# Last sliding-window layer: value products split by past and own keys, the last tile's scores in two bursts, its residual on two engines with one store, and new instruction orders

## The chip, the cores and the metric

One core of one Trainium2 chip runs the whole program. The metric is the device time of one execution in microseconds (us). The engines are named as in the profile: PE (TensorE, matrix products; PEld its weight loads), DVE (VectorE), ACT (ScalarE), POOL (GpSimd), SP (SyncE, which issues most DMAs).

## The reference

Four layers follow each other on x of 2048 tokens by 512 features, in bf16; each normalises x, computes an attention block and adds it to x. Layers 1 and 3 are a linear attention (A), layers 2 and 4 a softmax attention over a sliding window of 256 keys (B), both with 32 heads of 16 features. The last layer is a B layer:

```
def _B_ref(x, wqkv, wo):
    H = 32; Dh = D // H; W = 256
    q, k, v = ...                      # x @ wqkv, split by head
    scores = einsum("bhqd,bhkd->bhqk", q, k) * (Dh ** -0.5)
    mask = (idx[:, None] - idx[None, :] >= 0) & (idx[:, None] - idx[None, :] < W)
    p = _softmax(where(mask, scores, -1e9))
    return einsum("bhqk,bhkd->bhqd", p, v) ... @ wo

x = x + _A_ref(_layernorm(x), A_wqkv, A_wo)
x = x + _B_ref(_layernorm(x), B_wqkv, B_wo)
x = x + _A_ref(_layernorm(x), A_wqkv, A_wo)
x = x + _B_ref(_layernorm(x), B_wqkv, B_wo)
```

## The kernel before

The 2048 tokens are 16 tiles of 128. x stays in the on-chip memory (`xres`) through all four layers. In a B layer the loop of `middle` goes over the tiles j. For each tile it projects queries, keys and values some tiles ahead, and then works on key blocks: a tile has two blocks of 64 keys (2j and 2j + 1), and the 128 output partitions of a score matmul are the 64 keys of a block for two heads.

- `b_scores` (L623): one burst of eight score matmuls for two of the four head groups f and one key block b. The matmuls use a quarter of the rows of the array each (tile_position), so that a burst writes four accumulation banks. Keys of a tile meet the queries of the same and of the next tiles, so that the scores come out transposed, keys on partitions. Two ScalarE exponentials (L648) take the burst to `pb` or `vp` (the buffer `K.P`), and masks follow on DVE (L658) or POOL (L657). For tile 15, which has no later queries, a burst is 128 columns (b = 0) or 64 (b = 1) per head group.
- `b_far` (L682, exponentials L692, masks L702, L710, L711): the far edge of the window, for tiles with j + 2 < 16.
- `b_values` (L716, matmuls L731): value products of tile j, for h = 0 and 1, two steps "pv" of 24 matmuls each. A matmul takes 128 queries of one head pair against one key block, over up to six blocks: the two own ones first and then up to four past ones. The 34 output columns hold for each of two heads 16 features and a column for the softmax sum; a reciprocal (L742) and a multiplication (L743) give `o`.
- `b_out` (L748): transpose of `o` by a DMA (or, where `by_pe`, by TensorE), four products of 512 columns with `wBo` (L406), and the residual on DVE (L574); then a store of the tile (L849). The last tile has `b_last` (L755): transposes by TensorE in two halves (L766), products (L777), two half residuals on DVE (L783) and a store after each (L784).

The order of the instructions is not computed in the kernel. `place` (L92) reads a compressed table of numbers that gives, for every step, its rank, its engine where it may run on two, and its accumulation bank. `synchronise` puts in the semaphore waits. Every engine works through its own queue in this order.

## Time and profile before

| | |
|---|---|
| median of 3 runs | 407.9 us (407.73 to 408.55) |
| the profiled execution | 409.79 us; span 408.1 us |
| busy share of the span | PE 95%, ACT 84%, DVE 82%, PEld 64%, POOL 37% |
| last ACT exponential of the program | 397.99 + 1.87 us, the last of a row of four |
| granted TensorE clock, mean | 0.999 |

The span runs from the first to the last instruction; the time of an execution also has what lies around it. In the group rows, "busy, mean ns of one | idle before, releaser" is read as: the engine was busy for so long on this group, one instruction took so long, and it stood idle so long just before instructions of the group, mostly for the one named. In the timeline rows the first two numbers are start and length.

### The profile page before, as it was taken

To read this page: it belongs to the slowest core of one execution; us is meant where nothing else is said; L and a number is where in the kernel's file an instruction comes from. 1 tells how busy PE (TensorE), PEld (TensorE's weight loads), DVE (VectorE), ACT (ScalarE), POOL (GpSimd) and SP (SyncE) were. 2 spreads that over 40 slices of the span, in tenths; PEclk is the share of its full clock that TensorE was granted. 3 is DMA by queue.
4 is the path that set the end of the run, shared out by engine and by line. 5 is a ranking of instruction groups with operands and counts; after the bars stand their busy time and mean duration, and the time that the engine had idled before them with its cause. 6 is when DMAs were issued, how large, how long until landed. Compare 5 with 4: busy or idle time off the path is not lost.

```text
span 408.1 us, 18068 instructions
## 1 busy us (share of the span) xinstructions
PE 386.1 (95%) x7922; PEld 262.9 (64%) x7997; DVE 333.4 (82%) x758; ACT 341.3 (84%) x441; POOL 151.6 (37%) x246
## 2 busy tenths in 40 slices
PE   8999999998999999999999999999999999899895
PEld 4544776766575566565665777676767766576663
DVE  5998898979998898887857789988798768776774
ACT  3465569998999999999998345999899999999992
POOL 3555624443464455451742223132313223030351
PEclk9999999999999999999999999999999999999999
DMA  7934316333263535343232000345214433345352
GB/s 247 243 65 103 106 41 136 106 77 85 69 95 81 120 83 113 75 116 93 60 72 41 16 2 27 98 100 126 65 46 121 109 89 74 74 111 115 83 146 81
DMA packets 67654, 37.88 MB, mean 93 GB/s; under 512 B 48248, under 2 KB 62712, under 8 KB 67576
## 3 DMA queue, kind: packets, MB, share of 16 engines
q1 hardware_dynamic: 67184, 35.67, 36.6%
q8 instruction: 63, 1.03, 1.1%
q0 software_dynamic: 384, 1.05, 0.7%
q14 instruction: 15, 0.12, 0.1%
q10 hardware_dynamic: 8, 0.00, 0.0%
HBM read 6.29 MB, written 2.10 MB: 21 GB/s over the span
## 4 chain that ended last, share of the span: by engine, by line
PE 69%; ACT 12%; DVE 9%; DMA 5%; issue 2%; SPq 1%; ACTq 0%
PE ps L406 22%; PE ps L420 18%; PE ps L731 14%; ACT pb L648 9%; PE ps L638 7%; DMA xres<-in_A_x_dram 2%; PE ps L682 2%; DMA pb<-in_B_wqkv_dram 2%; DVE stats L367 1%; DVE vp L431 1%; PE ps L679 1%; ACT vp L648 1%; PE ps L457 1%; ACT pb L692 1%; DVE o L743 1%
## 5 line engine op out<-in xcount | busy, mean ns | idle before, releaser
L648 ACT ACTIVATE pb<-ps 128x1024 bf16<-128x1024 f32 (+3 forms) x224 | 198.4, 973 | 8.1 <-PE ps L638 6.6
L731 PEld LDWEIGHTS ps<-vB,pb 128*128 128x128 bf16 x2560 | 77.7, 96 | 11.2 <-issue 5.0
L731 PE MATMUL ps<-vB,pb 128*128 128x34 bf16 x2560 | 83.1, 177 | 1.0 <-issue 0.8
L420 PE MATMUL ps<-xT,wBp 128*128 128x128 bf16 x1024 | 68.8, 219 | 0.3 <-ACT pb L648 0.3
L420 PEld LDWEIGHTS ps<-xT,wBp 128*128 128x128 bf16 x1024 | 58.7, 98 | 10.6 <-issue 4.6
L710 POOL TENSOR_SCALAR_AFFINE_SELECT pb<-pb 128x1024 bf16<-128x1024 bf16 x35 | 40.4, 1155 | 64.0 <-DVE pb L702 37.2
L429 ACT ACTIVATE tE<-ps 128x512 bf16<-128x512 f32 x64 | 37.8, 605 | 24.6 <-PE ps L406 15.0
L692 ACT ACTIVATE pb<-ps 128x1024 bf16<-128x1024 f32 x50 | 49.3, 1052 | 2.1 <-PE ps L682 1.0
L657 POOL TENSOR_SCALAR_AFFINE_SELECT pb<-pb 128x512 bf16<-128x512 bf16 x50 | 33.7, 674 | 45.0 <-ACT pb L648 18.1
L574 DVE TENSOR_TENSOR xres<-ps,xres 128x512 bf16<-128x512 f32 x63 | 42.8, 682 | 9.3 <-PE ps L406 9.0
L638 PE MATMUL ps<-XQ,kB 32*128 32x256 bf16 (+2 forms) x1024 | 48.1, 262 | 2.2 <-ACT pb L648 0.8
L370 POOL TENSOR_TENSOR rs<-ve,negh 128x1 f32<-128x1 f32 x64 | 37.0, 578 | 32.1 <-DVE ve L369 27.5
L406 PE MATMUL ps<-wA,XQ 128*128 128x512 bf16 x179 | 45.9, 379 | 2.8 <-DMA XQ<-vp 0.8
L367 DVE BATCH_NORM_STATS2 stats<-xres 128x6 f32<-128x512 bf16 x64 | 43.7, 685 | 3.1 <-DMA xres<-in_A_x_dram 2.3
L420 PE MATMUL ps<-XQ,wA 128*128 128x128 bf16 x512 | 35.4, 219 | 0.1
L369 POOL TENSOR_SCALAR ve<-mv 128x1 f32<-128x1 f32 x45 | 11.3, 252 | 63.2 <-DVE mv L368 61.1
L420 PEld LDWEIGHTS ps<-XQ,wA 128*128 128x128 bf16 x512 | 30.5, 98 | 5.9 <-issue 0.7
L638 PEld LDWEIGHTS ps<-XQ,kB 32*128 32x128 bf16 x1024 | 15.4, 92 | 27.6 <-ACT pb L648 9.3
L742 DVE RECIPROCAL rc<-ps 128x16 f32<-128x16 f32 x64 | 16.1, 252 | 20.2 <-PE ps L731 19.7
L406 PE MATMUL ps<-wBv,xT 128*128 128x512 bf16 x108 | 30.1, 380 | 2.4 <-issue 1.3
L406 PE MATMUL ps<-wBo,oT 128*128 128x512 bf16 x103 | 28.5, 380 | 3.0 <-issue 1.8
L406 PE MATMUL ps<-M,XQ 128*128 128x512 bf16 x114 | 29.7, 380 | 1.3 <-issue 0.6
(116 smaller groups left out, 562.0 us busy)
## 6 DMA issues: line engine op xcount, KB each, us to landing
vB<-vS SPq DMA_DIRECT2D x64, 136.0 KB, 2.6
kB<-vp SPq DMA_DIRECT2D x64, 128.0 KB, 2.4
wA<-in_A_wqkv_dram SPq DMA_DIRECT2D x3, 512.0 KB, 5.2
xres<-in_A_x_dram SPq DMA_DIRECT2D x2, 512.0 KB, 4.8
pb<-in_B_wqkv_dram SPq DMA_DIRECT2D x1, 1024.0 KB, 8.6
out_dram<-xres POOLq DMA_DIRECT2D x8, 128.0 KB, 2.7
out_dram<-xres SPq DMA_DIRECT2D x7, 128.0 KB, 2.9
xres<-in_A_x_dram SPq DMA_DIRECT2D x3, 256.0 KB, 4.9
```

The source lines that it names most:

```text
L367: self.on("DVE", "stats", lambda e: e.bn_stats(K.stats[:, t, :], K.xres[:, t, :]), key, dve(512), rd=[("xres", t)], wr=[("stats", t)])
L370: self.pow = self.on("POOL", "pow", lambda e: e.tensor_tensor(K.rs[:, t, :], K.ve[:, t, :], K.negh[:], ALU.pow), key + 0.03, (640, 690), r ...
L406: m = e.matmul(K.ps(ps), lhs(c), rhs(c), start=c == 0, stop=c == 3)
L420: m = e.matmul(K.ps(ps)[:, f * P:(f + 1) * P], w(c, f), xT(c), start=c == 0, stop=c == 3)
L429: self.on("ACT", "E", lambda e: e.activation(K.tE[:, s, :], K.ps(ps), ACT.Exp, bias=0.0), key, act(512), wr=[("tE", s)], ps=[ps])
L574: self.on("DVE", "res", lambda e: e.tensor_tensor(K.xres[:, t, :], K.ps(po), K.xres[:, t, :], ALU.add), key, dve(512), rd=[("xres", t)], w ...
L638: m = e.matmul(K.ps(ps[gq])[:, ns * i:ns * i + ns], K.kB[rows, j % 4, 2 * f + b, :, :], K.XQ[rows, f, q:q + ns], start=True, stop=True, ti ...
L648: return e.activation(out(h, ns).rearrange("p (f g) c -> p f g c", f=n), i, ACT.Exp, bias=0.0, scale=0.25)
L657: return e.affine_select(out=x, in_=x, compare_op=ALU.is_ge, fill=0.0, base=1, pattern=[[0, 4 * n], [2, 64]], channel_multiplier=-1)
L692: return e.activation(o.rearrange("p (f g) b c -> p f g b c", g=2), i, ACT.Exp, bias=0.0, scale=0.25)
L710: return e.affine_select(out=x, in_=x, compare_op=ALU.is_ge, fill=0.0, base=-2, pattern=[[0, 16], [-2, 64]], channel_multiplier=1)
L731: m = e.matmul(K.ps(ps)[:, 34 * u:34 * u + 34], K.P((b // 2) % rp)[:, f, gq % 2 * 2 + gq // 2, o:o + P], K.vB[:, (b // 2) % 4, b % 2, r, : ...
```

## The change

Only the last layer changes. Its steps become:

- From tile 1 on the value products of two head groups are split in two each: those of the four past key blocks (16 matmuls) and those of the two own ones (8), in the same bank. The past part depends on the scores of earlier tiles alone (`b_split`).
- Tile 15's scores come in two bursts, one for each pair of head groups, with both key blocks side by side in a bank (192 columns for each group): two exponentials of 768 columns for each burst, and four masks, all on DVE (`b_scores_end`). Its own-key products are split by which of the two exponentials they need (`b_values_end`).
- In `b_last` the right half of x of tile 15 is added on TensorE, by a product with the identity, and copied out by ScalarE; the left half is added on DVE; one store of 128 KB follows both.
- `pe_last3` = 2: tile 14's `o` is also transposed by TensorE and no longer by a DMA.
- The table is new. Up to the last layer's first projections all engines have the same instructions in the same order as before; from there order, engines of copies and masks, and banks differ.

```
@@ -25,7 +25,7 @@
...
-    k_ao3=3.649, k_kv3=2.494, k_v3=-0.211, pe_first3=3, pe_last3=1, o_bke3=-0.456, o_res3=2.95,
+    k_ao3=3.649, k_kv3=2.494, k_v3=-0.211, pe_first3=3, pe_last3=2, o_bke3=-0.456, o_res3=2.95,
...
@@ -214,6 +214,7 @@
 
 LATE = 5
 FILL = 10
+SPLIT = 1
 
 
 def bass_view(x, free):
@@ -659,6 +660,39 @@
 
         self.g.add("mk", {"DVE": dve(256 * n, "2x"), "POOL": (600, 660)}, mk, key + 0.02, rd=[("P", sl, f, b, h) for f in fs for h in range(2)] + [("tri",)], wr=[("P", sl, f, b, 2) for f in fs])
 
+    def b_scores_end(self, j, fs, key):
+
+        K = self
+        ps = [Tile(1, "S") for _ in range(4)]
+        w = 3 * P // 2
+        span = lambda two, free: bass_view(K.PS[:, two[0].banks[0], :], free([512 * (two[1].banks[0] - two[0].banks[0]), 2]))
+
+        def put(e):
+            m = None
+            for i, f in enumerate(fs):
+                for b in range(2):
+                    c, q = w * i + 64 * (1 - b), P * j + 64 * b
+                    for gq in range(4):
+                        rows = slice(32 * gq, 32 * gq + 32)
+                        m = e.matmul(K.ps(ps[gq])[:, c:c + P - 64 * b], K.kB[rows, j % 4, 2 * f + b, :, :], K.XQ[rows, f, q:P * j + P], start=True, stop=True, tile_position=(32 * gq, 0))
+            return m
+
+        self.pe("s", put, key, 1, w * len(fs), mode=(32, 128), rd=[("kB", j % 4, 0), ("kB", j % 4, 1), ("XQ", j)], ps=ps)
+        sl = j % self.rp
+        for h in range(2):
+            def ex(e, h=h):
+                i = span(ps[2 * h:2 * h + 2], lambda x: [[w, 2], x, [1, w]])
+                o = bass_view(K.P(sl)[:, fs[0], h, 384:384 + w], [[1408, 4], [1, w]])
+                return e.activation(o.rearrange("p (f g) c -> p f g c", f=2), i, ACT.Exp, bias=0.0, scale=0.25)
+
+            self.on("ACT", "ex", ex, key + 0.01 * h, act(4 * w), wr=[("P", sl, f, b, h) for f in fs for b in range(2)], rd=[("P", sl, f) for f in fs], ps=[ps[2 * h], ps[2 * h + 1]])
+        for h in range(2):
+            def mk(e, h=h):
+                x = bass_view(K.P(sl)[:, fs[0], h, 384:448], [[1408, 4], [64, 2], [1, 64]])
+                return e.tensor_tensor(x, x, K.tri[:, 0, :].unsqueeze(1).unsqueeze(1).to_broadcast([P, 4, 2, 64]), ALU.mult)
+
+            self.on("DVE", "mk", mk, key + 0.02 + 0.01 * h, dve(512, "2x"), rd=[("P", sl, f, b, h) for f in fs for b in range(2)] + [("tri",)], wr=[("P", sl, f, b, 2, h) for f in fs for b in range(2)])
+
     def b_far(self, j, key):
 
         K = self
...
-    def b_values(self, j, h, key):
+    def b_whole(self, j, h, key, ps):
+
         K = self
         rp = self.rp
-        ps = Tile(1, K.cls)
...
+    def b_split(self, j, h, key, ps):
+
+        K = self
+        rp = self.rp
+        prior = [(2 * j - 1, 64), (2 * j - 2, 128), (2 * j - 3, 192), (2 * j - 4, 256)][:2 * j]
+        own = [(2 * j, 0), (2 * j + 1, -64)]
+        fs = (2 * h, 2 * h + 1)
+        parts = [(f, prior, f == fs[0], 0) for f in fs if prior] + [(f, own, f == fs[0] and not prior, 1) for f in fs]
+        for f, blocks, first, late in parts:
+            def put(e, f=f, blocks=blocks, first=first):
+                m = None
+                for gq in range(4):
+                    r = 4 * f + gq
+                    u = 4 * (f - 2 * h) + gq
+                    for i, (b, c) in enumerate(blocks):
+                        o = 384 * (b % 2) + c
+                        m = e.matmul(K.ps(ps)[:, 34 * u:34 * u + 34], K.P((b // 2) % rp)[:, f, gq % 2 * 2 + gq // 2, o:o + P], K.vB[:, (b // 2) % 4, b % 2, r, :], start=first and gq == 0 and i == 0, stop=blocks is own, skip_group_check=True)
+                return m
...
+            self.pe("pv", put, key - 0.4 * (1 - late) - 0.001 * (f % 2), 4 * len(blocks), 34, rd=rd, ps=[ps])
+
+    def b_values(self, j, h, key):
+        K = self
+        rp = self.rp
+        ps = Tile(1, K.cls)
+        if not (self.merged and j >= SPLIT):
+            self.b_whole(j, h, key, ps)
+        else:
+            self.b_split(j, h, key, ps)
         s = j % 2
         v = lambda: K.ps(ps)[:, 0:272].rearrange("p (u a d) -> p u a d", u=8, a=2)
         self.on("DVE", "rcp", lambda e: e.reciprocal(K.rc[:, s, h, :].rearrange("p (u a) -> p u a", a=2), v()[:, :, :, 16]), key + 0.02, dve(16, "recip"), wr=[("rc", s, h)], ps=[ps])
@@ -745,6 +814,51 @@
             v()[:, :, :, 0:16], K.rc[:, s, h, :].rearrange("p (u a) -> p u a", a=2).unsqueeze(3).to_broadcast([P, 8, 2, DH]), ALU.mult),
             key + 0.03, dve(256), rd=[("rc", s, h)], wr=[("o", s, h)], ps=[ps])
 
+    def b_values_end(self, j, h, key):
+
+        K = self
+        rp = self.rp
+        ps = Tile(1, K.cls)
+        fs = (2 * h, 2 * h + 1)
+        prob = lambda b, f, gq: K.P((b // 2) % rp)[:, f, gq % 2 * 2 + gq // 2, :]
+        val = lambda b, f, gq: K.vB[:, (b // 2) % 4, b % 2, 4 * f + gq, :]
+        for f in fs:
+            def put(e, f=f):
+                m = None
+                for gq in range(4):
+                    u = 4 * (f - 2 * h) + gq
+                    for b, c in ((2 * j - 4, 256), (2 * j - 3, 192), (2 * j - 2, 128), (2 * j - 1, 64)):
+                        o = 384 * (b % 2) + c
+                        m = e.matmul(K.ps(ps)[:, 34 * u:34 * u + 34], prob(b, f, gq)[:, o:o + P], val(b, f, gq), start=f == fs[0] and gq == 0 and b == 2 * j - 4, stop=False, skip_group_check=True)
+                return m
+            rd = []
+            for i in (j - 2, j - 1):
+                rd += [("P", i % rp, f)] + [("vB", i % 4, a, b) for a in range(2) for b in range(2)]
+                rd += [("P", i % rp, f, b, h_) for h_ in range(3) for b in (0, 1)]
...
+            self.pe("pv", put, key - 0.4 - 0.001 * (f % 2), 16, 34, rd=rd, ps=[ps])
+        for k in range(2):
+            def put(e, k=k):
+                m = None
+                for f in fs:
+                    for gq in (2 * k, 2 * k + 1):
+                        u = 4 * (f - 2 * h) + gq
+                        x = prob(2 * j, f, gq)
+                        e.matmul(K.ps(ps)[:, 34 * u:34 * u + 34], x[:, 448:576], val(2 * j, f, gq), start=False, stop=False, skip_group_check=True)
+                        m = e.matmul(K.ps(ps)[:, 34 * u:34 * u + 34], x[:, 320:448], val(2 * j + 1, f, gq), start=False, stop=True, skip_group_check=True)
+                return m
+            rd = [("vB", j % 4, a, b) for a in range(2) for b in range(2)]
+            for f in fs:
+                rd += [("P", j % rp, f)] + [("P", j % rp, f, b, k) for b in (0, 1)] + [("P", j % rp, f, b, 2, k) for b in (0, 1)]
+            self.pe("pv", put, key - 0.001 * (1 - k), 8, 34, rd=rd, ps=[ps])
...
     def b_out(self, j, key, by_pe):
         K = self
         s = j % 2
@@ -775,13 +889,14 @@
                     m = None
                     for f in (h, h + 2):
                         m = e.matmul(K.ps(po)[:, cs], K.oT[:, s, f, :], K.wBo[:, f, cs], start=f == 0, stop=f == 3, skip_group_check=True)
+                    if h == 0:
+                        m = e.matmul(K.ps(po)[:, 256:512], K.ident[:], K.xres[:, j, 256:512], start=False, stop=False, skip_group_check=True)
                     return m
 
-                self.pe("bout", put, key + 0.1 * h + 0.01 * (n or 0), 2, cs.stop - cs.start, rd=[("oT", s, h), ("wBo",)], ps=[po])
-        for n in range(2):
-            cs = slice(256 * n, 256 * n + 256)
-            self.on("DVE", "res", lambda e, cs=cs: e.tensor_tensor(K.xres[:, j, cs], K.ps(po)[:, cs], K.xres[:, j, cs], ALU.add), key + 0.2 + 0.1 * n, dve(256), rd=[("xres", j)], wr=[("xres", j, n)], ps=[po])
-            self.on("SP", "out", lambda e, cs=cs: e.dma_start(K.out[0, j * P:(j + 1) * P, cs], K.xres[:, j, cs]), key + 0.3 + 0.1 * n, (520, 2400), rd=[("xres", j, n)])
+                self.pe("bout", put, key + 0.1 * h + 0.01 * (n or 0), 2 if h else 2.5, cs.stop - cs.start, rd=[("oT", s, h), ("wBo",), ("xres", j), ("ident",)], ps=[po])
+        self.on("ACT", "res", lambda e: e.activation(K.xres[:, j, 256:512], K.ps(po)[:, 256:512], ACT.Copy), key + 0.2, act(256), rd=[("xres", j)], wr=[("xres", j, 1)], ps=[po])
+        self.on("DVE", "res", lambda e: e.tensor_tensor(K.xres[:, j, 0:256], K.ps(po)[:, 0:256], K.xres[:, j, 0:256], ALU.add), key + 0.2, dve(256), rd=[("xres", j)], wr=[("xres", j, 0)], ps=[po])
+        self.on("SP", "out", lambda e: e.dma_start(K.out[0, j * P:(j + 1) * P, :], K.xres[:, j, :]), key + 0.3, (520, 2400), rd=[("xres", j, 0), ("xres", j, 1)])
 
     def phase(self, ph):
 
@@ -831,12 +946,15 @@
             if j + 1 < T:
                 self.b_v(j + 1, (j + 1) % ring, base + j + 1 - par["k_v"])
             for f in (0, 2):
+                if last and j == T - 1:
+                    self.b_scores_end(j, [f, f + 1], base + j + f / 4)
+                    continue
                 for b in range(2):
                     self.b_scores(j, b, [f, f + 1], base + j + (f + b) / 4)
             if j + 2 < T:
                 self.b_far(j, base + j + 0.8)
             for h in range(2):
-                self.b_values(j, h, base + j + (h + 1) / 2 + par["k_pv"])
+                (self.b_values_end if last and j == T - 1 else self.b_values)(j, h, base + j + (h + 1) / 2 + par["k_pv"])
             if not last:
                 self.closing = [self.g.ops[-1]]
             k = base + j + 1 + par["k_wo"]
@@ -859,60 +977,61 @@
 
 
 TABLE = (
-    r"c-qxkW1u8i(hXg;ZQHhO+qP}nwr$(CZQGpb9`~2|YG!tOwtKf1f4;2B%&NE%anCssbzf%Hd*U9uXYRQJAV7HF!T>`kP!J9TG$e#X5E{Zm1V{`?ASon+<Y3^T",
...
+    r"c-qx@W1uWawsmYo?1;LyZCib9+qP|6-Pg8l+qP|6eQms~Q{6M&)3<wi-n{R}S5=vLYRAS}Yez<A)`{th;fw8y<5LP1sHncsid0CYRanK!s01pZ3Z=rS@G6l?",
...
```

The first place is TensorE's queue over the scores of tiles 14 and 15. Rows are equal instructions that follow each other; L638 (before), L639 and L677 (after) are score matmuls, L731, L791 and L832 value products, L406 and L407 output products, `pb` and `vp` the exponentials' buffers. Before:

```order
L638 MATMUL ps<-XQ,kB 128x256 x8
L406 MATMUL ps<-wBo,oT 128x512 x4
L731 MATMUL ps<-vB,pb 128x34 x24
L638 MATMUL ps<-XQ,kB 128x64 x8
L731 MATMUL ps<-vB,pb 128x34 x24
L638 MATMUL ps<-XQ,kB 128x128 x8
L731 MATMUL ps<-vB,pb 128x34 x48
L638 MATMUL ps<-XQ,kB 128x64 x8
L406 MATMUL ps<-wBo,oT 128x512 x2
L638 MATMUL ps<-XQ,kB 128x128 x8
```

After:

```order
L639 MATMUL ps<-XQ,kB 128x256 x8
L407 MATMUL ps<-wBo,oT 128x512 x2
L791 MATMUL ps<-vB,pb 128x34 x32
L677 MATMUL ps<-XQ,kB 128x128 x4
L677 MATMUL ps<-XQ,kB 128x64 x4
L677 MATMUL ps<-XQ,kB 128x128 x4
L677 MATMUL ps<-XQ,kB 128x64 x4
L791 MATMUL ps<-vB,pb 128x34 x64
L677 MATMUL ps<-XQ,kB 128x128 x4
```

The four small bursts of tile 15 stood between blocks of 24 and 48 value products; now the first of two comes after 32 products of tile 14's past keys, and 64 products, own and past, stand ahead of the second.

The second place is the end of DVE's queue: masks (L658; L692 after), reciprocals (L742; L856), divisions (L743; L857), residuals of a whole tile (L574; L575) and of half of tile 15 (L783; L898). Before:

```order
L658 TENSOR_TENSOR vp<-vp,tri 128x8x64
L742 RECIPROCAL rc<-ps 128x16
L743 TENSOR_TENSOR o<-ps,rc 128x8x2x16
L742 RECIPROCAL rc<-ps 128x16
L743 TENSOR_TENSOR o<-ps,rc 128x8x2x16
L574 TENSOR_TENSOR xres<-ps,xres 128x512 x2
L783 TENSOR_TENSOR xres<-ps,xres 128x256 x2
```

After:

```order
L692 TENSOR_TENSOR vp<-vp,tri 128x4x128 x4
L856 RECIPROCAL rc<-ps 128x16
L857 TENSOR_TENSOR o<-ps,rc 128x8x2x16
L856 RECIPROCAL rc<-ps 128x16
L857 TENSOR_TENSOR o<-ps,rc 128x8x2x16
L575 TENSOR_TENSOR xres<-ps,xres 128x512
L396 COPY oT<-ps 128x2x128
L575 TENSOR_TENSOR xres<-ps,xres 128x512
L898 TENSOR_TENSOR xres<-ps,xres 128x256
```

All four masks of tile 15 now stand together ahead of both reciprocals, a copy of the transposed second half of tile 15 has come between the two whole residuals, and one half residual has left for ScalarE.

The third place is the end of TensorE's queue (L731, L847, L848 value products, L766, L880 transposes, L777, L891 tile 15's output products, L893 the product with the identity). Before:

```order
L731 MATMUL ps<-vB,pb 128x34 x4
L777 MATMUL ps<-wBo,oT 128x512 x2
L766 MATMUL ps<-ident,o 128x128 x2
L406 MATMUL ps<-wBo,oT 128x512 x4
L777 MATMUL ps<-wBo,oT 128x256 x4
```

After:

```order
L848 MATMUL ps<-vB,vp 128x34
L407 MATMUL ps<-wBo,oT 128x512 x4
L880 MATMUL ps<-ident,o 128x128 x2
L407 MATMUL ps<-wBo,oT 128x512 x2
L880 MATMUL ps<-ident,o 128x128 x2
L407 MATMUL ps<-wBo,oT 128x512 x2
L891 MATMUL ps<-wBo,oT 128x512 x2
L893 MATMUL ps<-xres,ident 128x256
L891 MATMUL ps<-wBo,oT 128x256 x4
```

The output products of tile 13 (the first four of L407) have moved behind the last value products, and tile 15's first half of output products behind those of tile 14.

121 lines of the change are left out of this document (68 added, 53 removed).

## The prediction

> **What bounds the kernel now.** I read the page first, then the busy time by stretches, then the groups of one engine, then the engines' rows over the last ten microseconds.
>
> ```profile
> span 408.1 us, 18068 instructions
> PE 69%; ACT 12%; DVE 9%; DMA 5%; issue 2%; SPq 1%; ACTq 0%
> ```
>
> The chain of waits is mostly TensorE over the whole program, but only the last layer changes, so that layer has to be read alone. Its first score exponentials start at 256.8 us and its last one ends at 399.86 us. The busy time by stretches, with the columns named in the first line:
>
> ```profile
> core 0: us, PE busy (x) PEld busy (x) DVE busy (x) ACT busy (x) POOL busy (x), PEclk, DMA share, GB/s
> 256.80:290.00 33.20, 32.16 (x704) 22.61 (x710) 28.63 (x68) 31.98 (x42) 8.47 (x11) 1.00 0.41 104
> 290.00:340.00 50.00, 47.72 (x1212) 33.78 (x1220) 40.30 (x91) 46.15 (x59) 12.49 (x15) 1.00 0.35 87
> 340.00:399.86 59.86, 54.96 (x1610) 40.10 (x1620) 42.88 (x100) 57.85 (x73) 18.09 (x24) 1.00 0.44 104
> 399.86:408.10 8.24, 3.92 (x72) 2.51 (x70) 3.75 (x9) 0.77 (x2) 0.56 (x1) 0.96 0.28 80
> ```
>
> Up to 340 us TensorE (96%) and ScalarE (94%) are both nearly full. From 340 us ScalarE is busy 97% and TensorE 92%: the exponentials set the pace. Over the three stretches ScalarE is busy 135.98 of 143.06 us, so 7.1 us of idle time is all that an order can win there. The last 8.24 us belong to nobody: a chain of short steps. The ScalarE groups between 256.8 and 399.86 us say what the engine does and what it waits for:
>
> ```profile
> L648 ACT ACTIVATE pb<-ps 128x896 bf16<-128x896 f32 x88 | 74.6, 937 | 3.0 <-PE ps L638 3.0
> L692 ACT ACTIVATE pb<-ps 128x1024 bf16<-128x1024 f32 x22 | 21.7, 1045 | 1.3 <-PE ps L682 1.0
> L648 ACT ACTIVATE vp<-ps 128x896 bf16<-128x896 f32 x24 | 20.6, 944 | 1.0 <-PE ps L638 1.0
> L692 ACT ACTIVATE vp<-ps 128x1024 bf16<-128x1024 f32 x6 | 5.8, 1021 | 0.9 <-PE ps L682 0.8
> L648 ACT ACTIVATE pb<-ps 128x768 bf16<-128x768 f32 x4 | 3.1, 849 | 0.0
> L395 ACT ACTIVATE XQ<-ps 128x512 bf16<-128x512 f32 x5 | 3.1, 611 | 0.1
> L648 ACT ACTIVATE vp<-ps 128x512 bf16<-128x512 f32 x4 | 2.2, 595 | 0.2
> L648 ACT ACTIVATE vp<-ps 128x256 bf16<-128x256 f32 x4 | 1.4, 431 | 0.4 <-PE ps L638 0.4
> L395 ACT ACTIVATE vS<-ps 128x512 bf16<-128x512 f32 x2 | 1.3, 658 | 0.0
> L591 ACT ACTIVATE vp<-ps 128x512 bf16<-128x512 f32 x1 | 0.8, 762 | 0.0
> L548 ACT ACTIVATE rec<-recf 128x128 bf16<-128x128 f32 x2 | 0.6, 306 | 0.0
> ```
>
> Nearly all of the idle time, 3.0 + 1.3 + 1.0 + 0.9 + 0.4 = 6.6 us, is an exponential that waits for its burst of score matmuls (L638, L682). So what matters is how early TensorE reaches a burst, how many instructions ScalarE has, and how long the last chain is.
>
> **Part 1, the last tile's scores in two bursts.** Today the last tile has four bursts and eight exponentials, four of 512 columns and four of 256. They stand in these two ScalarE rows (start, length):
>
> ```profile
> 395.65 1.96 ACT L648 ACTIVATE vp<-ps 128x256 bf16<-128x256 f32 x4
> 397.99 1.87 ACT L648 ACTIVATE vp<-ps 128x256 bf16<-128x256 f32 x4 [0.39 <-PE ps L638]
> ```
>
> That is 1.96 + 1.87 = 3.83 us. They become four of 768 columns; the four of that size above took 3.1 us together. Gain 0.7 us, all of it on the engine that sets the pace. The wait of 0.39 us between the groups I leave in: in the new order TensorE has 64 value products between the two new bursts. Forty-eight of them take 1.37 us by the row below, so 64 take about 1.75 us, while ScalarE has at that point one 1024-column and two 768-column exponentials before it, about 2.5 us. The burst and the mask that the last of these products wait for use up the rest, and 0.2 to 0.4 us of waiting remains.
>
> ```profile
> 396.40 1.37 PE L731 MATMUL ps<-vB,pb 128*128 128x34 bf16 x48
> ```
>
> **Part 2, copies that change engines.** In the new order ScalarE loses, between the 9th and the 85th exponential of the layer, two query copies net (0.61 each), one value copy (0.66) and two of the reciprocals' copies (0.31 each) and gains one key copy (0.76): 1.22 + 0.66 + 0.61 - 0.76 = 1.7 us less. All of this lies before 340 us or little after it, where TensorE is as full as ScalarE, so it need not show. Its bounds are 0 and 1.7 us; I take 0.7, since TensorE sets the pace there about as often as ScalarE. VectorE pays: about four us more with the masks that also move to it, on 111.8 busy us of 143.1. That is 81% instead of 78%, so it is hidden as long as no burst waits for it.
>
> **Part 3, value products split.** The number of products does not change: 24 for a group of four heads before, 16 + 8 after. Only their place does. Products of past keys no longer wait for the tile's own exponentials and masks, and blocks of 24 to 48 between two bursts become blocks of 8 to 64. No row prices that. The upper bound of the gain is the 6.6 us of burst waits; the loss has no bound in the trace, and the nearest row is the same 6.6 us once more. Since the two orders hold the bursts and the projections in nearly the same places, I take 0.5 us of gain.
>
> **Part 4, the end.** The rows after the last exponential (399.86 us), first VectorE, then TensorE, ScalarE and the SP queue:
>
> ```profile
> 399.89 0.43 DVE L658 TENSOR_TENSOR vp<-vp,tri 128x512 bf16<-128x512 bf16 x1 [1.37 <-ACT vp L648]
> 401.92 0.26 DVE L742 RECIPROCAL rc<-ps 128x16 f32<-128x16 f32 x1 [0.97 <-PE ps L731]
> 402.21 0.42 DVE L743 TENSOR_TENSOR o<-ps,rc 128x256 bf16<-128x256 f32 x1
> 403.88 0.69 DVE L574 TENSOR_TENSOR xres<-ps,xres 128x512 bf16<-128x512 f32 x1 [0.65 <-PE ps L406]
> 404.49 0.87 DVE L783 TENSOR_TENSOR xres<-ps,xres 128x256 bf16<-128x256 f32 x2
> ...
> 400.38 0.21 PE L731 MATMUL ps<-vB,vp 128*128 128x34 bf16 x2
> 401.63 0.25 PE L731 MATMUL ps<-vB,pb 128*128 128x34 bf16 x4
> 402.69 0.28 PE L766 MATMUL ps<-ident,o 128*128 128x128 bf16 x2 [0.32 <-DVE o L743]
> 402.81 1.03 PE L406 MATMUL ps<-wBo,oT 128*128 128x512 bf16 x4
> 403.68 0.60 PE L777 MATMUL ps<-wBo,oT 128*128 128x256 bf16 x4
> ...
> 403.01 0.38 ACT L395 ACTIVATE oT<-ps 128x256 bf16<-128x256 bf16 x1 [1.31 <-PE ps L766]
> ...
> 403.26 1.67 SPq L849 DMA_DIRECT2D out_dram<-xres  x2
> 404.97 0.92 SPq L784 DMA_DIRECT2D out_dram<-xres  x2
> ```
>
> Now, counted from the last exponential: the mask, then 48 products (400.38 to 401.88), then reciprocal and division, ready at +2.77; then one residual, the transposes, eight products with the output weights and three more residual steps, the last ready at 405.36, that is +5.5; then the second half store.
>
> After: the mask ends at about +0.55 (three masks queue up behind each other), and only 8 of the last 32 own-key products wait for it, 0.2 us and 0.2 until their result is there: +1.0. Two pairs of reciprocal and division follow each other on VectorE, 0.71 us each by the rows 401.92 to 402.63, from +0.8: ready at +2.2, so 0.55 earlier. Then VectorE has the residual of tile 13 (0.69), a copy of the transposed tile (about 0.38, as ScalarE's), the residual of tile 14 (0.69) and one half residual (0.43): +4.4. TensorE has, from +1.0, eight output products of 512 columns for tiles 13 and 14 (1.03 for four in the row 402.81, so 2.0), two transposes, two products of 512 and one of 256 and four of 256 (0.60): its last result comes at about +4.2, and ScalarE's half residual (about 0.4) ends at +4.6. So the last residual is ready 0.9 us earlier. The extra product with the identity (256 columns) lies beside VectorE's residuals and costs nothing; uncovered it would cost 0.1 us.
>
> The store becomes one of 128 KB instead of two of 64 KB, of which only the second is at the end. Medians from issue to landing:
>
> ```profile
> out_dram<-xres SPq DMA_DIRECT2D x7, 128.0 KB, 2.9
> xres<-in_A_x_dram SPq DMA_DIRECT2D x2, 128.0 KB, 2.2
> out_dram<-xres SPq DMA_DIRECT2D x2, 64.0 KB, 1.7
> ```
>
> The bounds are 0 (as a half) and 1.2 us more (2.9 against 1.7, most of those stores sent beside other traffic). I take 0.5, the 128 KB load's 2.2 us, since the queues are quieter at the end. The end then gains 0.9 - 0.5 = 0.4 us, with bounds 0.9 and -0.3.
>
> [...]
>
> **The sum.** 0.7 + 0.7 + 0.5 + 0.4 = 2.3 us less. The profiled execution took 409.79 us (span 408.1), 1.9 us above the median of 407.9; it would become 407.5, and the median 405.6. A measurement of this kernel can tell about 0.2% (0.8 us) from no change, so 407.1 to 408.7 counts as the same.
>
> **The rivals.**
>
> *Slower: bursts queue behind own-key products.* The own-key blocks wait for a VectorE mask (0.43 us plus VectorE's queue), and TensorE takes its queue in order. Where such a block stands ahead of a burst, the burst waits for the mask, and ScalarE for the burst. The 64 products before the last burst are such a place, and each tile has one. It decides where mask and block together take longer than the exponentials that ScalarE still has in hand, about two of 0.83 us (74.6 / 88 is 0.85). At 0.3 us on each of 14 tiles it costs 4.2 us, against 1.8 of gain from parts 1, 2 and 4: 410.3. For it: VectorE gets busier. Against it: today's blocks wait for the same masks, in larger pieces.
>
> *No change: the gains do not reach the end.* TensorE hides the copies and the splitting, and the store costs the full 1.2 us: 0.7 + 0.9 - 1.2 = 0.4 us, 407.5.
>
> *Much faster.* Past-key products fill TensorE's waits so well that half of the 6.6 us of burst waits goes: 3.3 in place of 0.5, 402.8.
>
> That the first three layers run as now is certain from the order: up to the last layer's first projections every engine has the same instructions in the same places.
>
> **Numbers.** The forecast (404.3 to 407.1) has 0.52, much faster (below 404.3) 0.15, no change 0.14, slower 0.19. Faster is 0.52 + 0.15 = 0.67. Below 402.6 I leave 0.05 and above 409.3 about 0.12, which takes in the ends of all unknown terms short of a slower rival at its full price: range 402.6 to 409.3.
>
> **What would show it.** Right: four exponentials of 768 columns on tile 15 in about 3.1 us; ScalarE's idle time by bursts near 6 us over the layer; the last exponential 1.9 us earlier than 399.86; the last store issued 4.6 us behind it. Wrong: burst waits of 8 us or more in the ScalarE groups, which is the slower rival; a last exponential that is no earlier (the copies and the splitting are hidden); a last store that takes 2.9 us; or VectorE named as what TensorE's bursts wait for.

## The result and the profile after

The changed kernel takes 409.73 us (median of 20 runs, 408.10 to 411.96) against 408.45 us for the kernel before, run beside it: ratio 1.0034, 95% interval 1.0019 to 1.0048. It is slower, by about 1.3 us, where I forecast 2.3 us of gain; the time lies above my range. Its profiled execution took 409.66 us and that of before 409.79 us, so these two executions hardly differ as wholes. They have to be read stage by stage.

The page of the changed kernel, its span and its chain of waits:

```profile
span 407.9 us, 18149 instructions
...
PE 84%; ACT 7%; DVE 5%; DMA 2%; issue 1%; DVEq 0%; ACTq 0%
```

TensorE's share of the chain rose from 69 to 84%. One execution does not give this share well: over the profiled executions of the kernels below it is 69 to 81% with the bulk of before and 77 to 87% with the new bulk ("bulk" means the last layer up to tile 14's last exponential).

TensorE's busy time can't be compared between these two profiles. The lines of the engines on the two pages, first of before, then of after:

```profile
PE 386.1 (95%) x7922; PEld 262.9 (64%) x7997; DVE 333.4 (82%) x758; ACT 341.3 (84%) x441; POOL 151.6 (37%) x246
PE 395.3 (97%) x8002; PEld 264.7 (65%) x8002; DVE 336.6 (83%) x761; ACT 340.8 (84%) x434; POOL 151.3 (37%) x250
```

The profile of the changed kernel has as many matmuls as weight loads (PEld), 8002 of each; that of before has 7922 matmuls beside 7997 weight loads, so I take it that the records of 75 matmuls are missing there. Up to 256.8 us, ahead of the last layer's scores, where both kernels have 4381 weight loads, before shows 4332 matmuls and the changed kernel 4380, and TensorE seems busy 247.36 us before and 253.21 us after. So the 92% and 96% of TensorE in the prediction are too low, and a TensorE that looks busier after the change shows nothing.

Stretches at fixed times also cut the two programs at different places. The pairs of far exponentials (L692 before, L726 after) mark the same place in both. These are the busy times from the first pair to the ninth, from there to the last pair, and from there to the last exponential, first of before, then of after:

```profile
260.33:340.78 80.45, 77.34 (x1897) 55.24 (x1912) 66.25 (x152) 75.49 (x96) 20.41 (x25) 1.00 0.37 92
340.78:383.05 42.27, 38.93 (x1121) 28.13 (x1125) 30.65 (x71) 41.81 (x51) 9.84 (x13) 1.00 0.44 99
383.05:399.86 16.81, 15.25 (x427) 11.24 (x429) 11.45 (x27) 15.27 (x23) 8.25 (x12) 1.00 0.45 124
```

```profile
260.56:340.66 80.10, 78.32 (x1911) 55.42 (x1910) 67.52 (x151) 74.70 (x91) 20.60 (x29) 1.00 0.39 87
340.66:384.29 43.63, 40.73 (x1129) 28.75 (x1128) 32.66 (x76) 42.33 (x50) 11.77 (x15) 1.00 0.46 105
384.29:399.33 15.04, 14.72 (x424) 11.13 (x422) 11.04 (x27) 14.79 (x20) 6.23 (x8) 1.00 0.45 119
```

Read the second number, the length: 0.35 us won in the first part, 1.36 lost in the middle, 1.77 won in the last (0.75 of that is a stall in before's execution, see below). The last exponential ends at 399.33 us instead of 399.86. In the middle part ScalarE does nothing but the same 50 exponentials in both kernels, and in before it is busy 41.81 of 42.27 us: little was left for a new order to win there. Its groups in that part, of before and of after, say what was lost:

```profile
L648 ACT ACTIVATE pb<-ps 128x896 bf16<-128x896 f32 x32 | 26.8, 958 | 0.3 <-PE ps L638 0.3
L692 ACT ACTIVATE pb<-ps 128x1024 bf16<-128x1024 f32 x9 | 9.0, 1065 | 0.2 <-PE ps L682 0.2
L648 ACT ACTIVATE vp<-ps 128x896 bf16<-128x896 f32 x8 | 6.7, 941 | 0.0
L692 ACT ACTIVATE vp<-ps 128x1024 bf16<-128x1024 f32 x2 | 1.9, 1020 | 0.0
```

```profile
L649 ACT ACTIVATE pb<-ps 128x896 bf16<-128x896 f32 x32 | 27.0, 936 | 0.6 <-PE ps L639 0.4
L726 ACT ACTIVATE pb<-ps 128x1024 bf16<-128x1024 f32 x8 | 7.8, 1038 | 0.7 <-PE ps L716 0.7
L649 ACT ACTIVATE vp<-ps 128x896 bf16<-128x896 f32 x8 | 6.7, 924 | 0.0
L726 ACT ACTIVATE vp<-ps 128x1024 bf16<-128x1024 f32 x2 | 1.9, 1020 | 0.2 <-PE ps L716 0.2
```

Waiting for bursts grew from 0.5 to 1.5 us there (0.6 + 0.7 + 0.2).

The lengths of the first two parts hold beyond this pair. In the six profiled executions with the bulk of before in both parts (before, split_in_place, tail_only and three of new_end, all described below) the first part took 80.24 to 80.45 us and the middle 42.00 to 42.64; in the six with the new bulk (after, after_again, bulk_only and three of two_banks) they took 79.25 to 80.10 and 43.18 to 44.04. On average 0.7 us is won in the first part and 1.2 lost in the middle. The last part can't be compared in this way, since stalls and drops of the clock make it 15.0 to 18.2 us long.

The end, in the changed kernel (exponentials of tile 15, a stall, the residuals and the store):

```profile
396.04 1.52 ACT L686 ACTIVATE vp<-ps 128x768 bf16<-128x768 f32 x2
397.82 1.51 ACT L686 ACTIVATE vp<-ps 128x768 bf16<-128x768 f32 x2 [0.26 <-PE ps L677]
...
399.58 0.84 PE L832 MATMUL ps<-vB,pb 128*128 128x34 bf16 x27 [0.57 <-issue]
...
404.20 0.38 ACT L897 ACTIVATE xres<-ps 128x256 bf16<-128x256 f32 x1 [1.57 <-PE ps L891]
404.62 0.42 DVE L898 TENSOR_TENSOR xres<-ps,xres 128x256 bf16<-128x256 f32 x1 [0.70 <-ACT xres L897]
405.07 0.34 SPq L899 DMA_DIRECT2D out_dram<-xres  x1
```

The four exponentials take 3.03 us, as forecast. But the two half residuals follow each other: VectorE's waits for ScalarE's (0.70 us, releaser L897). Both read halves of one accumulation bank, `po`, and the kernel orders every pair of users of a bank, readers too. From the last exponential to the last residual it is 405.04 - 399.33 = 5.7 us; before it was 5.5, and I had written 4.6.

### The profile page after: what moved, and what is told of

The parts are those of the page before. It is cut to its first block, busy times and chain, and to the rows that moved or that the text cites. A ratio compares the mean times of both kernels' runs of the same rounds, so it can differ in the third digit from the quotient of the medians.

```text
span 407.9 us, 18149 instructions
## 1 busy us (share of the span) xinstructions
PE 395.3 (97%) x8002; PEld 264.7 (65%) x8002; DVE 336.6 (83%) x761; ACT 340.8 (84%) x434; POOL 151.3 (37%) x250
## 4 chain that ended last, share of the span: by engine, by line
PE 84%; ACT 7%; DVE 5%; DMA 2%; issue 1%; DVEq 0%; ACTq 0%
PE ps L407 28%; PE ps L421 19%; PE ps L791 9%; PE ps L639 8%; PE ps L765 7%; ACT pb L649 5%; PE ps L482 3%; PE ps L716 2%; DMA xT<-xn 2%; PE ps L713 1%; ACT vp L649 1%; PE ps L1104 1%; PE ps L458 1%; PE ps L544 1%; DVE XQ L564 1%
## 5 line engine op out<-in xcount | busy, mean ns | idle before, releaser
L744 POOL TENSOR_SCALAR_AFFINE_SELECT pb<-pb 128x1024 bf16<-128x1024 bf16 x33 | 38.5, 1168 | 37.2 <-DVE pb L745 12.0
L726 ACT ACTIVATE pb<-ps 128x1024 bf16<-128x1024 f32 x50 | 49.0, 1045 | 3.6 <-PE ps L716 2.8
L658 POOL TENSOR_SCALAR_AFFINE_SELECT pb<-pb 128x512 bf16<-128x512 bf16 x50 | 33.7, 674 | 48.8 <-ACT pb L649 22.3
L575 DVE TENSOR_TENSOR xres<-ps,xres 128x512 bf16<-128x512 f32 x63 | 42.9, 683 | 9.3 <-PE ps L407 8.7
L639 PE MATMUL ps<-XQ,kB 32*128 32x256 bf16 (+3 forms) x992 | 47.4, 264 | 2.2 <-ACT pb L649 0.5
L407 PE MATMUL ps<-wA,XQ 128*128 128x512 bf16 x192 | 48.5, 380 | 0.2 <-DVE XQ L564 0.2
L370 POOL TENSOR_SCALAR ve<-mv 128x1 f32<-128x1 f32 x51 | 13.3, 260 | 90.5 <-DVE mv L369 88.7
L765 PEld LDWEIGHTS ps<-vB,pb 128*128 128x128 bf16 x1472 | 40.5, 96 | 6.7 <-issue 2.4
L765 PE MATMUL ps<-vB,pb 128*128 128x34 bf16 x1472 | 42.9, 177 | 0.3 <-DVE pb L745 0.2
L791 PE MATMUL ps<-vB,pb 128*128 128x34 bf16 x1024 | 37.5, 178 | 0.4 <-issue 0.3
L791 PEld LDWEIGHTS ps<-vB,pb 128*128 128x128 bf16 x1024 | 33.7, 96 | 6.2 <-issue 3.9
L407 PE MATMUL ps<-wBv,xT 128*128 128x512 bf16 x128 | 34.2, 380 | 0.2 <-ACT pb L649 0.2
L407 PE MATMUL ps<-wBo,oT 128*128 128x512 bf16 x124 | 33.2, 380 | 0.3 <-ACT vp L649 0.3
L407 PE MATMUL ps<-M,XQ 128*128 128x512 bf16 x128 | 32.7, 380 | 0.0
```

The source lines that it names most:

```text
L407: m = e.matmul(K.ps(ps), lhs(c), rhs(c), start=c == 0, stop=c == 3)
L575: self.on("DVE", "res", lambda e: e.tensor_tensor(K.xres[:, t, :], K.ps(po), K.xres[:, t, :], ALU.add), key, dve(512), rd=[("xres", t)], w ...
L639: m = e.matmul(K.ps(ps[gq])[:, ns * i:ns * i + ns], K.kB[rows, j % 4, 2 * f + b, :, :], K.XQ[rows, f, q:q + ns], start=True, stop=True, ti ...
L726: return e.activation(o.rearrange("p (f g) b c -> p f g b c", g=2), i, ACT.Exp, bias=0.0, scale=0.25)
L744: return e.affine_select(out=x, in_=x, compare_op=ALU.is_ge, fill=0.0, base=-2, pattern=[[0, 16], [-2, 64]], channel_multiplier=1)
L765: m = e.matmul(K.ps(ps)[:, 34 * u:34 * u + 34], K.P((b // 2) % rp)[:, f, gq % 2 * 2 + gq // 2, o:o + P], K.vB[:, (b // 2) % 4, b % 2, r, : ...
```

## The experiments

My theories now: (1) the shared bank takes the gain of the end; (2) the new order of the bulk costs time because it feeds ScalarE's bursts later where ScalarE is full; against them, that the split products or the new end themselves cost. First the change in pieces, with the two halves in two banks as a fourth kernel:

```
tail_only        order of before with whole products up to tile 14's last exponential, then the new end
bulk_only        new order and split up to there, then the old end
split_in_place   order of before; every step of 24 products cut into 16 + 8, back to back
two_banks        the changed kernel with
-        po = Tile(1, K.cls)
+        po = [Tile(1, K.cls) for _ in range(2)]     # products, residual of half n on po[n]
```

> The order before up to the last exponential of tile 14, with whole value products, and from there the new end: two score bursts for tile 15, its residual on two engines, one store, tile 14 transposed by TensorE, in the new order. If the bulk (split and new order of tiles 0 to 13) is what costs time, this is 0.3 to 0.8 us faster than the kernel before, since four exponentials of 768 columns replace eight. If the new end costs it, it is as slow as the changed kernel, 1.0 to 1.5 us above the kernel before.

> The other half of the change: split value products and the new order up to the last exponential of tile 14, then the end as before (four bursts, two half residuals on VectorE, two stores). If the bulk costs time, 1.3 to 2 us above the kernel before; if the end does, within 0.4 us of it.

> The order before without any move: each step of 24 value products is only cut in two steps (16 of past keys, 8 of own), one right behind the other. If the cutting itself costs TensorE time (more steps, another order of the products), 0.5 us or more above the kernel before; if only the places matter, within 0.3 us of it, or up to 0.5 us faster because the first part no longer waits for the tile's own masks.

> The changed kernel with the two halves of the last residual in two accumulation banks, so that VectorE's half does not wait for ScalarE's. If the serial pair of residuals is a cost on the last chain, the VectorE half starts about 0.7 us earlier and the run is about 0.4 us faster than the changed kernel (about 409.3); if the store or another step ends last, no change. Either way it stays above the kernel before if the bulk is what costs time.

Measured against before on one chip: tail_only 0.9994 (0.9976 to 1.0011), bulk_only 1.0037 (1.0020 to 1.0054), split_in_place 0.9993 (0.9975 to 1.0010), two_banks 0.9996 (0.9975 to 1.0018). Only bulk_only is clear of no change. tail_only was to be 0.3 to 0.8 us faster than before if the bulk is what costs time; it measures 0.25 us, and its interval allows both that gain and none. two_banks, which I expected above before, is level with it. Splitting the products by itself costs nothing that can be measured (at most 0.1%). The new order of the bulk with the old end is as slow as the whole change. bulk_only has a seam where the two orders meet, so its size is not to be trusted by itself. In two_banks the residuals lie beside each other:

```profile
401.84 0.42 DVE L898 TENSOR_TENSOR xres<-ps,xres 128x256 bf16<-128x256 f32 x1
402.06 0.38 ACT L897 ACTIVATE xres<-ps 128x256 bf16<-128x256 f32 x1 [1.57 <-PE ps L891]
402.51 0.34 SPq L899 DMA_DIRECT2D out_dram<-xres  x1
```

Its last exponential ended at 397.70, so the last residual is ready 4.74 us later, near the forecast 4.6. Theory 1 holds in part: by these rows the bank cost some 0.4 us (5.71 less the stall of 0.57 is 5.14, against 4.74), and VectorE no longer waits for ScalarE. It is not the whole loss, as bulk_only has the old end.

Next, which engine sets the pace, and the good end on the good bulk:

```
after_again  the changed kernel, unaltered
new_end      order of before with whole products to tile 14's last exponential (SPLIT = 14), new end, two banks
pe_less      before, with   if self.merged and len(blocks) == 6: blocks = blocks[:5]
             (224 products of the farthest key block are left out, at 1.37 / 48 us each 6.4 us of TensorE)
act_less     before, with one far exponential in two over 512 columns instead of 1024
             (key block b = 1 is left out, 14 x 0.43 = 6 us of ScalarE; 0.43 is 1.02 us for 1024 columns less 0.60 for 512)
```

> The changed kernel once more, unaltered, beside the next three on one chip. If the change really costs time, 0.2 to 0.5% above the kernel before again; if the difference hangs on the chip or on stalls that come and go, within 0.2% of it.

> The order before up to the last exponential of tile 14 with whole value products, then the end of the changed kernel as it stands there, with the products of tile 14 split too (so that 64 and not 96 stand ahead of the last burst), and the last residual in two banks. If the end of the change is sound and the bulk costs what it wins, this is 1.0 to 1.9 us faster than the kernel before. If TensorE's total work sets the end in any case, within 0.5 us of it.

> The kernel before, which leaves out the value products of the farthest past key block in the last layer: 4 of 24 matmuls in each step of tiles 2 to 15, 224 matmuls or about 6 us of TensorE work. If ScalarE's exponentials set the pace of the layer, 0 to 2 us faster; if TensorE does, 4 to 6 us faster.

> The kernel before with half of one of the two far-edge exponentials of every tile left out in the last layer (512 of 1024 columns, 14 times), about 6 us of ScalarE work. If ScalarE's exponentials set the pace, 3 to 6 us faster; if TensorE does, 0 to 2 us.

Measured: after_again 1.0012 (0.9985 to 1.0040), new_end 0.9971 (0.9949 to 0.9993), pe_less 0.9969 (0.9945 to 0.9992), act_less 0.9977 (0.9956 to 0.9998). after_again by itself is not clear of no change. Six microseconds of TensorE's work taken away bring 0.31% or 1.3 us, and six of ScalarE's bring 0.23% or 0.9 (at most 2.2 and 1.8 us by the intervals). In act_less the time comes back as waiting for bursts, as the ScalarE groups over the layer say (3.0 and 1.6 us stood there before):

```profile
L648 ACT ACTIVATE pb<-ps 128x896 bf16<-128x896 f32 (+2 forms) x96 | 80.9, 926 | 6.5 <-PE ps L638 6.2
L648 ACT ACTIVATE vp<-ps 128x896 bf16<-128x896 f32 (+2 forms) x32 | 24.1, 822 | 2.1 <-PE ps L638 1.8
```

That holds in the middle part too. ScalarE is 1.3 us less busy there in act_less than in before, and the part is no shorter (42.49 against 42.27 us):

```profile
341.35:383.84 42.49, 38.86 (x1121) 28.23 (x1125) 30.59 (x71) 40.47 (x51) 9.87 (x13) 1.00 0.48 98
```

So neither engine alone is the bound of the layer: of what is taken from one of them about a fifth (1.3 / 6.4) or a seventh (0.9 / 6) is passed on, and by the intervals at most a third. That the two engines hold each other up is how I read this; no run shows it apart from other causes. new_end is faster than before (0.9971) and than the changed kernel beside it (after_again, 1.0012).

Then I looked for the place of the loss, with the bulk's two halves from different orders, cut about the ninth far pair (340 us), always with the new end in two banks:

```
early_after   new order and split to about 340 us, then the order of before with whole products
early_before  the other way round
```

> The changed order with split products up to the eighth pair of far-edge exponentials (about 340 us), then the order of before with whole products, then the new end with its two halves in two banks. If the later stages are where the changed order loses (from 340 to 384 us the five stages took 43.6 us in the changed kernel and 42.3 in the kernel before), this takes the good half of each: ratio 0.996 to 0.997, the stages from the eighth to the last pair of far exponentials about 42.4 us, and no slower than the kernel with the whole order of before and the new end (0.997). If the work is only moved between stages, the last stage (from the last far pair to the last exponential) goes from 15.0 back to 16.3 us, and the time is that of the other order: the five stages 42.4 and the last one 16.3, the sum from the first exponential to the last within 0.3 us of both.

> The order of before with whole products up to the eighth pair of far-edge exponentials, then the changed order with split products, and the new end with its two halves in two banks. If the changed order loses in the later stages: the five stages there take 43.4 us or more, and the ratio is 0.999 to 1.001, worse than its counterpart by 0.3% or more. If the work is only moved: the five stages take 43.4 us, the last one 15.0 instead of 16.3, and this kernel and its counterpart agree within 0.15%.

> The kernel with the order of before, whole products and the new end with two banks, once more: 0.997 as the first time if the new end is worth 1 us and the order of the bulk is what costs it; about 0.9995 if the first time was a kinder draw of the stalls.

> The changed kernel with the two halves of the last residual in two banks, once more, beside the others on the same chip: 0.9996 as the first time, so 0.25% behind the one with the order of before, if the bulk's new order costs about 1 us; level with it if the bulk's order is worth nothing either way.

Measured on one chip: early_after 1.0011 (0.9993 to 1.0029), early_before 1.0054 (1.0034 to 1.0073), new_end_b 0.9991 (0.9974 to 1.0008), two_banks_b 1.0010 (0.9992 to 1.0027). I had expected 0.996 to 0.997 for early_after and 0.999 to 1.001 for early_before; both came out slower, and neither mixture is as good as new_end. In all six runs of early_before the mean granted clock was 0.995 or 0.996 (see the last section). early_after loses 9.31 us against 7.9 in the stage that holds the seam (333.01 to 342.32), so the mixtures don't tell the size; but behind its seam the middle part took 42.56 us in the order of before. The two kernels without a seam do tell the place. The same three parts, new_end_b first, then two_banks_b:

```profile
260.26:340.55 80.29, 79.14 (x1912) 55.03 (x1910) 66.15 (x152) 75.36 (x96) 20.45 (x25) 1.00 0.37 92
340.55:382.55 42.00, 39.51 (x1127) 28.11 (x1125) 30.63 (x71) 41.81 (x50) 9.85 (x13) 1.00 0.48 96
382.55:398.02 15.47, 14.93 (x425) 11.04 (x423) 12.02 (x29) 14.92 (x20) 7.43 (x11) 1.00 0.51 141
```

```profile
260.17:339.94 79.77, 78.36 (x1911) 55.47 (x1910) 67.49 (x151) 74.80 (x92) 20.65 (x29) 1.00 0.41 87
339.94:383.98 44.04, 40.73 (x1129) 28.77 (x1128) 32.64 (x76) 42.38 (x51) 11.79 (x15) 1.00 0.47 103
383.98:399.01 15.03, 14.74 (x425) 11.14 (x424) 11.03 (x27) 14.77 (x20) 6.24 (x8) 1.00 0.45 121
```

The new order wins 0.5 us ahead of the ninth pair and loses 2.0 in the middle, of which 0.5 is a stall at 345 us that belongs to this execution. ScalarE's waits for bursts in that middle part are, in new_end_b and in two_banks_b:

```profile
L726 ACT ACTIVATE pb<-ps 128x1024 bf16<-128x1024 f32 x8 | 7.9, 1053 | 0.2 <-PE ps L716 0.2
```

```profile
L649 ACT ACTIVATE pb<-ps 128x896 bf16<-128x896 f32 x32 | 27.0, 932 | 0.8 <-PE ps L639 0.6
L726 ACT ACTIVATE pb<-ps 128x1024 bf16<-128x1024 f32 x9 | 8.8, 1035 | 0.6 <-PE ps L716 0.6
L649 ACT ACTIVATE vp<-ps 128x896 bf16<-128x896 f32 x8 | 6.7, 923 | 0.0
L726 ACT ACTIVATE vp<-ps 128x1024 bf16<-128x1024 f32 x2 | 1.9, 1020 | 0.4 <-PE ps L716 0.4
```

Theory 2 has its place and its sign in the middle part: 0.2 us of waiting in the order of before, 1.8 in the new one (some 0.5 of it behind that stall). Its size is another matter: 0.7 won ahead of it and 1.2 lost there leave 0.5 us, and in the last part new_end_b took 15.47 us and two_banks_b 15.03.

Last, are the engines of the copies to blame, or the order? The 25 steps that changed engine are put on the other side's engines, with the new end in two banks:

```
new_engines  new_end with the changed kernel's engines for copies of projections, far masks, reciprocals' copies
old_engines  two_banks with before's engines for them
```

> The order of before with whole products and the new end in two banks, but with the steps that changed engine (query, key and value copies, far masks, copies of reciprocals) on the changed kernel's engines. If taking copies from ScalarE to VectorE is the cost, because TensorE's next bursts or projections then wait for a busier VectorE, this is 0.15% or more slower than its neighbour without them. If the copies are worth what I forecast, 0.7 us faster; if both ScalarE and TensorE set the pace, level within 0.1%.

> The changed kernel's order and split products with the end in two banks, but those steps on the engines of before. If the engines are the cost, this comes within 0.1% of the kernel with the order of before; if the order with its split products is, it stays 0.15 to 0.25% behind, level with the changed order on its own engines or up to 0.1% slower.

> Order of before, whole products, new end in two banks, for the third time, as the neighbour of the other three: 0.997 to 0.999 of the kernel before.

> The changed kernel with two banks for the third time: 0.9995 to 1.001 of the kernel before and 0.15 to 0.25% behind the order of before with the same end. If instead it is level with it here, the earlier difference was scatter between executions and the bulk's order is worth nothing either way.

Measured: new_engines 1.0068 (1.0046 to 1.0089), old_engines 1.0214 (1.0190 to 1.0238), new_end_c 0.9981 (0.9965 to 0.9997), two_banks_c 1.0017 (0.9998 to 1.0035). Both mixtures are far worse than their neighbours new_end_c and two_banks_c, by 3.9 and 7.9 us where I had written of 0.15 to 0.25%: an order fits its own engines. So the bulk's loss can't be put on engines or on order alone, and that stays open. What new_engines shows is the cost of moving copies and far masks to VectorE in an order that wasn't made for it: other VectorE steps come later, and TensorE waits for them. Some of its waits in the last layer that new_end_b does not have (us in total, times, longest; masks at L736, a value copy at L396, a residual at L575, a reciprocal at L811):

```profile
PE ps L765 <- DVE vp L736: 0.6, 1, 0.6
PE ps L765 <- DVE pb L736: 0.6, 1, 0.6
PE ps L639 <- DVE vS L396: 0.6, 1, 0.6
...
PE ps L639 <- DVE xres L575: 0.5, 1, 0.5
...
PE ps L639 <- DVE rc L811: 0.5, 1, 0.5
```

## Why the prediction was wrong

The balance by ratios: the new end in two banks on the old bulk gives 0.9971, 0.9991, 0.9981, a mean of -0.19% or 0.8 us of gain (two of the three intervals exclude no change). The new bulk with the same end gives 0.9996, 1.0010, 1.0017, so the bulk's new order costs 0.25, 0.19 and 0.36%, 1.1 us. The first of these three compares runs of two chips; the other two pairs ran side by side, and without the runs whose mean clock is 0.996 or less both give 0.8 us. The changed kernel itself gave 1.0034 and 1.0012, on average 0.15% (0.6 us) behind two_banks; this term compares different chips and is the least sure. The sum, -0.8 + 1.1 + 0.6 = 0.9 us slower, is the mean of the two measurements (1.3 and 0.5) by the way the terms are made, and so it confirms nothing.

Two steps of the prediction failed: the 0.5 us of gain in part 3, in whose place the bulk with its new places and engines costs about 1.1 us, and the two halves side by side in part 4, which ran one after the other. Why the new bulk feeds the bursts later in the middle stays open.

- *"From 340 us the exponentials set the pace."* ScalarE is full there (41.81 of 42.27 us), but it doesn't set the pace alone: with less for ScalarE to do (act_less) the part took 42.49 us. TensorE's 92% was read from a profile with missing records; in new_end_b, which has the order of before there and every record, TensorE is busy 39.51 of 42.00 us (94%) in the middle and 14.93 of 15.47 (97%) in the last part. Over the layer ScalarE's savings were passed on at about a seventh. I also drew the wrong conclusion: a part at 99% can win almost nothing by a new order and can lose.
- *Part 1* was right in size, 3.83 to 3.03 us. The wait before the second pair of exponentials stayed (0.26 us, forecast 0.2 to 0.4).
- *Part 2*, 0.7 us. The copies that left ScalarE all lie ahead of the ninth far pair, as I said; ScalarE is 0.8 us less busy there (75.49 to 74.70, forecast 1.7), and TensorE is busy 78.32 of 80.10 us. The part became 0.35 us shorter in the first pair of profiles and 0.7 on average, the size that I took; that is partly luck, since the new places of the products are in it too and no run parts them. The gain didn't reach the end, since the middle part lost more. VectorE's price was hidden, as forecast: TensorE's longest waits for it are 0.6, 0.6 and 0.5 us in the changed kernel, and 0.6, 0.5 and 0.5 before. In new_engines, with the order of before, it was not.
- *Part 3*, 0.5 us of gain taken from nothing but "nearly the same places". This is the step with the largest error: splitting by itself changes nothing that can be measured, and the new bulk, whose new places can't be told from its new engines, costs about 1.1 us by the ratios. My "slower" rival had the right symptom, bursts that come late, at the right size per wait (0.24 to 0.45 us for the far bursts of the middle part), but not on each of 14 tiles. That own-key products behind a mask are what holds them up was not shown. One burst that waits for VectorE does so in both orders (a far burst behind a key copy, 0.6 us in each).
- *Part 4*, 0.4 us of gain. The last residual was to come 4.6 us behind the last exponential and came 5.7 us behind it. I gave the two halves to two engines and let them run side by side, without looking at how the kernel orders users of one bank. Mended, it was 4.74. The store I over-priced: from its issue to the end of the span it took 407.9 - 405.07 = 2.83 us, against 408.1 - 405.43 = 2.67 us for the half store of before, whose issue at 405.43 follows from the row of two stores in the prediction (404.97 + 0.92 less 0.46 for one). So 128 KB instead of 64 KB cost about 0.16 us here and not 0.5; over all profiled executions the means are 2.79 us (2.69 to 2.89, thirteen) and 2.68 us (2.61 to 2.78, five), a step of 0.1 us. The median of 2.9 us from issue to landing that I reckoned with is mostly of stores sent at a busier time: five of the seven were issued before 396 us, and the DMA engines' share was 0.40 from 256.8 to 399.86 us against 0.28 from there to the end.

## What to carry to other kernels

Before giving two halves of a last step to two engines, see what orders the users of the memory between them: halves in one bank ran one after the other here (VectorE's waited 0.70 us for ScalarE's), and a second bank brought them side by side (401.84 and 402.06 us). A gain on one engine has to be set against the next-busy engine of the same stretch (of 6 us less for ScalarE 0.9 us came through here), and before TensorE's busy time is read, its matmul records have to be counted against its weight loads (7922 against 7997 in before). Where the waiting engine was already at 99% of a stretch (ScalarE, 41.81 of 42.27 us), a new order had 0.46 us to win there and lost 1.36 in the first pair of profiles; the new end on the old order (new_end: 0.9971, 0.9991, 0.9981) came out ahead of both kernels.

## What the runs showed of the hardware

*Stalls of TensorE without a releaser.* In the middle of a step TensorE stands for 0.2 to 1.3 us, put down to "issue", at nearly the same places of the program (about 361, 386 and, with the new end, 399.6 us) in some executions and not in others; two_banks shows none at the second place (TensorE busy 3.94 of 4 us from 384 to 388) and at most 0.26 us at the first (busy 1.74 of 2 us from 358 to 360). In the two executions shown here the weight loads stand still at the same time (0.83 us ahead of 385.37 in before, 0.67 us ahead of 399.58 in the changed kernel), so these two are not missing records. From the first place to the second TensorE has 634 weight loads in before, bulk_only and new_end_c alike, and from the second to the third 380 in new_end_c and after_again, though the orders differ. So a place seems to go with the count of TensorE's instructions and not with a step of the program; no run tests this. The one of before that stands in its last part:

```profile
385.36 0.20 PE L731 MATMUL ps<-vB,pb 128*128 128x34 bf16 x2 [0.75 <-issue]
```

In the changed kernel one lies on the last chain, at 399.58 us (0.57 us, above). Its cause isn't shown; no experiment was made on it.

*A clock that drops in the middle.* In five of the profiled executions (bulk_only, early_after, early_before, old_engines, new_end_c) the granted clock falls once between 300 us and the end of the last layer's scores. Summed over stretches of 2 us, what is missing to the full clock comes to 1.70 to 1.72 us in each, 0.26 x 2 + 0.50 x 2 + 0.10 x 2 = 1.72 in early_before. Its middle stretch shows 0.50; if the clock stands there all through, a drop lasts an estimated 1.72 / 0.50 = 3.4 us. The stretches around it in early_before and in bulk_only, each with a lull of TensorE ahead of the drop:

```profile
340.00:344.00 4.00, 2.63 (x128) 2.14 (x128) 3.33 (x9) 3.50 (x5) 0.84 (x3) 1.00 0.26 68
344.00:346.00 2.00, 2.00 (x69) 1.61 (x66) 1.16 (x4) 1.74 (x3) 0.00 (x0) 0.74 0.03 4
346.00:348.00 2.00, 2.00 (x54) 1.61 (x51) 1.03 (x4) 1.76 (x3) 0.00 (x0) 0.50 0.13 29
348.00:350.00 2.00, 2.00 (x28) 1.27 (x27) 1.19 (x3) 1.84 (x3) 0.00 (x0) 0.90 0.68 49
```

```profile
384.00:388.00 4.00, 3.18 (x108) 2.58 (x105) 1.98 (x5) 2.84 (x4) 1.72 (x2) 1.00 0.39 124
388.00:390.00 2.00, 1.83 (x19) 0.62 (x18) 0.81 (x4) 1.73 (x3) 0.00 (x0) 0.55 0.33 70
390.00:392.00 2.00, 2.00 (x64) 1.54 (x56) 1.73 (x4) 1.51 (x2) 0.03 (x1) 0.60 0.52 109
```

The clock is the third number from the right. TensorE was busy 2.63 of 4 us ahead of the first drop and 3.18 of 4 ahead of the second; in tail_only 3.01 of 4 at the same place (384 to 388) was followed by none, and in early_after 3.01 of 4 was followed by one. So the length of the lull alone doesn't decide. What does was not shown. Executions with a mean clock of 0.996 or less, which is about what such a drop makes (1.7 of 408 us is 0.4%), were 11 of 126 of before, 4 of 36 of new_end (with its repeats), 2 of 24 of tail_only and split_in_place, 20 of 80 of the kernels with the whole new bulk, 3 of 12 of early_after, 3 of 10 of new_engines, none of 24 of pe_less and act_less, and all 12 of early_before and old_engines. So the share goes with the order here, and why isn't shown. By these counts the drops are an estimated (20/80 - 17/186) x 1.7, about 0.3 us of the bulk's mean loss.
